# Weight rebuild through the idle accumulator bank, scaled v of the first batch on ScalarE, key low parts on VectorE

## The chip, the cores and the metric

The kernel runs on one core of a Trainium2 chip. The metric is the device time of one execution in microseconds (us); the kernel before takes 1162.75 us, the median of 3 runs (1162.2 to 1163.17). The engines are called PE (matmul), DVE (VectorE), ACT (ScalarE), POOL (GpSimd) and SP, whose queue here issues every DMA.

## The reference

Two stages. The weights reach the kernel as 64-bit numbers, all else as float32; it keeps precision by splitting numbers into a high and a low 16-bit part.

```python
q_pool = q.reshape(B, H, S // 2, 2, D).mean(axis=3)          # B=8, H=8, S=1152, D=64
scores = matmul(q_pool, k.T) / sqrt(D)                        # 576 x 1152 per head
x = softmax(scores) @ v                                       # heads side by side: (8, 576, 512)
x_prev = x shifted by one row
xk = mu_k * x + (1 - mu_k) * x_prev;  xr = mu_r * x + (1 - mu_r) * x_prev
out = sigmoid(xr @ w_r) * (maximum(xk @ w_k, 0) ** 2 @ w_v)   # w_k 512 x 1024, w_v 1024 x 512, w_r 512 x 512
```

## The kernel before, in words

**Attention.** There are 64 heads, eight to a batch, and six blocks of 96 pooled queries to a head: 384 blocks. Each has its scores in one of three PSUM tiles `s0` to `s2`. A block runs round a loop: nine score matmuls against the key's high and low parts (L462), the maximum over keys (DVE, L469), its transpose (PE, L472), the second maximum (DVE, L475), the shift spread by a small matmul (PE, L477), written into the query's spare row (ACT, L480), nine matmuls that add the rest and the shift (L486), and exp into `pf` (ACT, L492), which frees the PSUM tile. POOL then takes the low half of `pf` into `pl` (L494).

Five *windows* of 128 queries a head multiply `pf` and `pl` with `vt` and `vb` (L513, L515, L520) into one PSUM bank. DVE divides by the sum (L535 to L538); after an odd head PE turns both heads (L550) and ACT copies them out to `xt` (L553). The bank is `a`; with `ALT`, odd heads of the first batch use bank `f`, which is otherwise the accumulator of the feed-forward stage.

**Preparation of a head.** Keys: ACT rounds them (`kn`, L415), the rest is the low part (L418), by POOL for the first `KN_POOL` = 8 heads and by DVE for the others; a transposing DMA makes `ks1` of them. Values: ACT and DVE make `vt` (L428, L431), POOL makes the scaled copy `vb` (L434). Queries of two heads at a time: L382 to L389.

**Weights.** The three matrices arrive as 64-bit numbers in 20 pieces of 512 columns (`st`, two buffers). A piece is rebuilt to float32 and split: ACT takes the exponent and high mantissa (`ex`, L580) and the low mantissa bits (`em`, L587), DVE shifts and joins them (L590), DVE joins the sign (L598), ACT rounds (L600), POOL takes the rest (L601). All pieces are needed by the first batch's feed-forward.

**Feed-forward.** After each batch, tiles of 256 rows: mixing (L633 to L644), products of high and low parts (L665) in bank `f`, and in the last batch in all banks; activations (L692 to L720) and the output. The products of one batch fill PE while the next batch's attention runs.

**Order.** Nothing is issued as it is written. Every operation is recorded by `op` with its engine, a duration, what it reads and writes, a due time (`key`), and for DVE and POOL whether it needs the way to SBUF that both use (`port`). `Issue.run` then plays the record, with durations stretched by `LATE` and latencies by `SLACK`, and fixes one order for each engine; engines run in this order. A change of a duration, a due time or an engine thus moves instructions everywhere. Weights are recorded ahead of all blocks and windows, so whoever writes bank `f` later waits for what the weights did in it.

Of the kernel before, what the change touches and what calls it, by code (L numbers as in the profile page):

```python
# [256 lines left out]
def kernel(  # L257
# [145 lines left out]
    def prep(n, key):  # L403
# [37 lines left out]
    def block(n, j, i, t):  # L441
# [27 lines left out]
        op("DVE", 0.967, lambda: nc.vector.tensor_reduce(mxz, grid(0, NC).rearrange("p c q -> p q c"),  # L469
                                                         axis=AX.X, op=ALU.max),  # L470
           r=[("s", z)], w=[("mx", z)], key=t)
        op("PE", 0.057, lambda: nc.tensor.matmul(s[0:QN, 0:P], mxz, identb, start=False, stop=False,  # L472
                                                 skip_group_check=True),
# [5 lines left out]
           r=[("mb", z)], w=[("s", z)], key=t + O_MAX)  # L479
        op("ACT", 0.133, lambda: nc.scalar.activation(qlo[QN:QN + 1], s[QN:QN + 1, 0:QN], AF.Prelu,  # L480
                                                      scale=1.0 - EPS, alpha=(1.0 + EPS) / (1.0 - EPS)),
# [10 lines left out]
        op("ACT", NC * QN / 1200 + 0.051, lambda: nc.scalar.activation(  # L492
            pf[:, :, rows], grid(0, NC), AF.Exp, bias=SHIFT, scale=0.125 / (2.0 * SQ)), r=[("s", z)], w=[("pf", j)], key=t + O_EXP)
        op("POOL", NC * QN / 1000 + 0.12, lambda: nc.gpsimd.tensor_scalar(  # L494
            pl[:, :, rows], half(pf, U16, 0)[:, :, rows], LO, 1.0, op0=ALU.mult, op1=ALU.mult),
           r=[("pf", j)], w=[("pl", j)], key=t + O_REST)

    def window(n, w, t):
# [57 lines left out]


    def weights(n, w, kc, key, step):
        cols = w.shape[1]
        wv = w.bitcast(I32).rearrange("(c p) (f t) -> c p f t", p=P, t=2)  # L560
        for c in range(kc):
            for f in range(0, cols, 512):
# [17 lines left out]
                op("ACT", 0.48, lambda e=e, wh=wh: nc.scalar.activation(e, wh.bitcast(F32), AF.Abs, scale=2.0 ** -111),  # L580
                   r=[ks], w=[ke], key=key)
# [227 lines left out]
```

## Time and profile before

| what | value |
|---|---|
| runs | 1162.2, 1162.75, 1163.17 us |
| profiled execution: time, span | 1164.27 us, 1162.5 us |
| granted PE clock, mean | 0.997 |
| PE, DVE, ACT, POOL busy, share of span | 96%, 78%, 76%, 47% |
| PE's tenths in the first six of 40 slices (29 us each) | 4, 8, 8, 7, 7, 9, and 9 from there to the last but one |

Each row of a group names line, engine, operation, output and inputs by the program's names, count, busy time in us and mean in ns, then the idle time of the engine just ahead of these instructions and what ended it. A row of a stretch gives busy time and, in brackets, the number of instructions of each engine. Rows of consecutive instructions can overlap a little, and a busy PE isn't PE at its peak, since matmuls are pipelined.

### The profile page before, as it was taken

The page shows a single profiled execution, that of the slowest core. Times are in us where ns is not written, and L with a number is a line of the kernel's source. Part 1 is how long each engine was busy: PE and PEld are TensorE (multiplying, and loading weights), DVE is VectorE, ACT ScalarE, POOL GpSimd, SP SyncE. Part 2 cuts the span into 40 slices and gives each one's busy share as a digit, 9 for nine tenths or more (in the row PEclk, how much of TensorE's full clock was granted, in tenths as well). Part 3 has the DMA queues.
Part 4 walks back from the last instruction along what each step waited for, and adds up shares of the span by engine and source line. Part 5 has one row for each costly group of instructions (what it writes and reads, how often), then busy time and mean ns, then how long its engine had stood idle before and what let it go on. Part 6 is the DMA issues. An engine that isn't in the chain of part 4 may idle for free.

```text
span 1162.5 us, 45688 instructions
## 1 busy us (share of the span) xinstructions
PE 1111.6 (96%) x19504; PEld 926.0 (80%) x19504; DVE 908.2 (78%) x1791; ACT 888.7 (76%) x1838; POOL 550.0 (47%) x565
## 2 busy tenths in 40 slices
PE   4887799999999999999999999999999999999998
PEld 3776687978788887988788888979797978888565
DVE  6898878888888878888888878787888788774530
ACT  4988797887878788778877787878778778765743
POOL 4787554544445453544444453535354545443111
PEclk9999999999999999999999999999999999999999
DMA  9956663565545363564355536455554445310000
GB/s 233 219 143 175 155 135 78 134 130 126 129 99 114 94 143 98 134 123 106 90 109 120 132 81 145 85 117 115 113 123 86 95 112 93 70 30 10 20 19 28
DMA packets 222380, 126.69 MB, mean 109 GB/s; under 512 B 157664, under 2 KB 194528, under 8 KB 222176
## 3 DMA queue, kind: packets, MB, share of 16 engines
q1 hardware_dynamic: 222176, 123.77, 47.1%
q8 instruction: 152, 2.49, 0.9%
q14 instruction: 52, 0.43, 0.1%
HBM read 67.11 MB, written 9.44 MB: 66 GB/s over the span
## 4 chain that ended last, share of the span: by engine, by line
PE 85%; ACT 6%; DVE 3%; DMA 2%; issue 2%; POOL 1%; SPq 0%; DVEq 0%; ACTq 0%
PE f L665 33%; PE s L462 11%; PE s L486 11%; PE a L520 6%; PE a L515 6%; PE a L513 6%; PE s L665 4%; ACT pf L492 2%; PE s L472 2%; PE a L665 2%; DVE mx L469 1%; PE s L477 1%; PE a L550 1%; DMA st<-in_moe_w_k_dram 1%; ACT qT L480 1%
## 5 line engine op out<-in xcount | busy, mean ns | idle before, releaser
L494 POOL TENSOR_SCALAR pl<-pf 128x864 f16<-128x864 uint16 x384 | 385.0, 1003 | 405.4 <-ACT pf L492 378.3
L469 DVE TENSOR_REDUCE mx<-s 128x96 f16<-128x864 f32 x384 | 401.5, 1054 | 102.7 <-PE s L462 59.9
L492 ACT ACTIVATE pf<-s 128x864 int32<-128x864 f32 x384 | 337.4, 890 | 70.5 <-PE s L486 45.8
L462 PE MATMUL s<-qT,ks 128*128 128x96 f16 x3456 | 221.2, 207 | 28.6 <-DMA qT<-qn 15.1
L462 PEld LDWEIGHTS <-ks 128*128 128x128 f16 x3456 | 185.5, 99 | 54.6 <-issue 22.9
L515 PE MATMUL a<-vt,pf 128*128 128x64 f16 x2700 | 227.6, 194 | 0.0
L513 PE MATMUL a<-vt,pf 128*128 128x65 f16 x2700 | 227.2, 193 | 0.0
L486 PE MATMUL s<-qT,ks 128*128 128x96 f16 x3456 | 214.5, 207 | 7.2 <-ACT qT L480 6.7
L513 PEld LDWEIGHTS <-pf 128*128 128x128 f16 x2880 | 204.1, 99 | 6.0 <-ACT pf L492 0.4
L486 PEld LDWEIGHTS <-ks 128*128 128x128 f16 x3456 | 180.9, 98 | 28.5 <-issue 7.7
L515 PEld LDWEIGHTS <-pf 128*128 128x128 f16 x2880 | 194.8, 98 | 7.8 <-issue 0.3
L480 ACT ACTIVATE qT<-s 1x96 f16<-1x96 f32 x384 | 91.9, 243 | 99.8 <-PE s L477 87.6
L475 DVE TENSOR_REDUCE mb<-s 96x1 f16<-96x128 f32 x384 | 108.6, 285 | 57.9 <-PE s L472 53.3
L520 PE MATMUL a<-vb,pl 128*128 128x65 f16 x2700 | 143.4, 193 | 0.5 <-POOL pl L494 0.5
L665 PE MATMUL f<-xhk,wk_hi 128*128 128x256 f16 x496 | 135.1, 272 | 1.3 <-ACT xt L553 0.8
L665 PE MATMUL f<-xhk,wk_lo 128*128 128x256 f16 x496 | 135.1, 272 | 0.0
L665 PE MATMUL f<-xlk,wk_hi 128*128 128x256 f16 x496 | 135.1, 272 | 0.0
L520 PEld LDWEIGHTS <-pl 128*128 128x128 f16 x2880 | 121.8, 98 | 7.9 <-POOL pl L494 1.2
L696 POOL TENSOR_TENSOR gl<-g 128x512 f16<-128x512 f32 x72 | 78.5, 1090 | 100.7 <-ACT g L694 98.3
L665 PEld LDWEIGHTS <-wk_hi 128*128 128x128 f16 x1152 | 106.2, 98 | 11.6 <-issue 1.5
L472 PE MATMUL s<-identb,mx 128*96 128x128 f16 x384 | 87.1, 227 | 4.9 <-DVE mx L469 4.5
L665 PE MATMUL f<-wv_hi,g 128*128 128x512 f16 x240 | 90.9, 379 | 0.3 <-ACT ex L713 0.2
(101 smaller groups left out, 1990.2 us busy)
## 6 DMA issues: line engine op xcount, KB each, us to landing
kr<-in_k_dram SPq DMA_DIRECT2D x64, 288.0 KB, 3.3
vr<-in_v_dram SPq DMA_DIRECT2D x64, 288.0 KB, 3.1
qr<-in_q_dram SPq DMA_DIRECT2D x32, 320.0 KB, 3.7
ks<-ks SPq DMA_DIRECT2D x64, 144.0 KB, 2.8
out_dram<-em SPq DMA_DIRECT2D x36, 256.0 KB, 2.4
qr<-in_q_dram SPq DMA_DIRECT2D x32, 256.0 KB, 3.4
st<-in_moe_w_k_dram SPq DMA_DIRECT2D x8, 512.0 KB, 4.9
st<-in_moe_w_v_dram SPq DMA_DIRECT2D x8, 512.0 KB, 4.1
```

Source lines behind the costliest of these rows:

```text
L462: nc.tensor.matmul(cols(c, c + 1), ks1[hp][:, c, :], qhi, start=(c == c0), stop=False, skip_group_check=True)
L469: op("DVE", 0.967, lambda: nc.vector.tensor_reduce(mxz, grid(0, NC).rearrange("p c q -> p q c"), axis=AX.X, op=ALU.max), r=[("s", z)], w=[ ...
L472: op("PE", 0.057, lambda: nc.tensor.matmul(s[0:QN, 0:P], mxz, identb, start=False, stop=False, skip_group_check=True), r=[("mx", z)], w=[( ...
L475: op("DVE", 0.199, lambda: nc.vector.tensor_reduce(mbz[0:QN], s[0:QN, 0:P], axis=AX.X, op=ALU.max), r=[("s", z)], w=[("mb", z)], key=t + O ...
L480: op("ACT", 0.133, lambda: nc.scalar.activation(qlo[QN:QN + 1], s[QN:QN + 1, 0:QN], AF.Prelu, scale=1.0 - EPS, alpha=(1.0 + EPS) / (1.0 - ...
L486: nc.tensor.matmul(cols(c, c + 1), ks2[hp][:, c, :], qlo, start=False, stop=True, skip_group_check=True)
L492: op("ACT", NC * QN / 1200 + 0.051, lambda: nc.scalar.activation(pf[:, :, rows], grid(0, NC), AF.Exp, bias=SHIFT, scale=0.125 / (2.0 * SQ) ...
L494: op("POOL", NC * QN / 1000 + 0.12, lambda: nc.gpsimd.tensor_scalar(pl[:, :, rows], half(pf, U16, 0)[:, :, rows], LO, 1.0, op0=ALU.mult, o ...
L513: nc.tensor.matmul(bank[:, a0:a0 + VN], half(pf, F16, 1)[:, c, rows], vt[jv][:, c, D:D + VN], start=(w == 0 and c == 0), stop=False, skip_ ...
L515: nc.tensor.matmul(bank[:, a0:a0 + D], half(pf, F16, 1)[:, c, rows], vt[jv][:, c, 0:D], start=False, stop=False, skip_group_check=True)
L520: nc.tensor.matmul(bank[:, a0:a0 + VN], pl[:, c, rows], vb[jv][:, c, 0:VN], start=False, stop=(c == NC - 1), skip_group_check=True)
L665: nc.tensor.matmul(ps, terms[i][0], terms[i][1], start=(first and i == 0), stop=(i == last), skip_group_check=True)
```

## The change

It is one edit of the numbers and engines that the order is made from.

- *Rebuild* (`DEC_K`, `DEC_RV` from "D" to "S"): ACT writes the first part into bank `f` (`f_b`) instead of `ex`; DVE shifts and joins in place there (L607 in the new numbering), and joins the sign from `st` and `f` into `ex` (L610). Each of the two DVE instructions so has one operand in PSUM and one in SBUF, and both are recorded as not needing the common way. There were two `ex` buffers; there is one bank `f`.
- *Window sums* (`ALT` from 1 to 0): all heads use bank `a`.
- *Key low parts* (`KN_POOL` from 8 to 0): by DVE for all heads.
- *Scaled v* (`VB_ACT` = 8): by ACT for the first eight heads.
- *Order*: `LATE` 0.08 to 0.04, `SLACK` 0.1 to 0.05, and most of the recorded durations a little longer. All engines' orders come out anew; the instructions on PE are the same in number and kind.

```diff
--- before.py
+++ after.py
@@ -46,10 +46,12 @@
-LATE, SLACK = 0.08, 0.1
-KN_POOL, VT_POOL, XL_POOL = 8, 0, 0
-DEC_K, DEC_RV = "D", "D"
-ALT = 1
+LATE, SLACK = 0.04, 0.05
+KN_POOL, VT_POOL, XL_POOL = 0, 0, 0
+DEC_K, DEC_RV = 'S', 'S'
+ALT = 0
+PL_ENG, PL_N = (), 0
+VB_ACT = 8
 QSPLIT = 1
@@ -431,9 +433,13 @@
-        op("POOL", 0.75, lambda: nc.gpsimd.tensor_scalar(
-            vb[j][:, :, 0:D], vr[i], SV, VLO, op0=ALU.mult, op1=ALU.mult),
-           r=[("vr", i)], w=[("vb", j)], key=key + 4)
+        if n < VB_ACT:
+            op("ACT", NC * D / 1200 + 0.093, lambda: nc.scalar.activation(
+                vb[j][:, :, 0:D], vr[i], AF.Copy, scale=SV * VLO), r=[("vr", i)], w=[("vb", j)], key=key + 4)
+        else:
+            op("POOL", 0.75, lambda: nc.gpsimd.tensor_scalar(
+                vb[j][:, :, 0:D], vr[i], SV, VLO, op0=ALU.mult, op1=ALU.mult),
+               r=[("vr", i)], w=[("vb", j)], key=key + 4)
@@ -463,13 +469,13 @@
-            op("PE", (c1 - c0) * 0.0424, lambda c0=c0, c1=c1: scores(c0, c1),
+            op("PE", (c1 - c0) * 0.0430, lambda c0=c0, c1=c1: scores(c0, c1),
...
-        op("ACT", 0.133, lambda: nc.scalar.activation(qlo[QN:QN + 1], s[QN:QN + 1, 0:QN], AF.Prelu,
+        op("ACT", 0.153, lambda: nc.scalar.activation(qlo[QN:QN + 1], s[QN:QN + 1, 0:QN], AF.Prelu,
@@ -577,20 +589,49 @@
                 dec = DEC_K if n == "k" else DEC_RV
+                if dec in "STU":
+                    ep, kf = f_b.bitcast(I32), ("f",)
+                    pt = dec == "U"
+                    op("ACT", 0.52, lambda wh=wh: nc.scalar.activation(f_b, wh.bitcast(F32), AF.Abs, scale=2.0 ** -111),
+                       r=[ks], w=[kf], key=key)
+                    op("ACT", 0.565, lambda mi=mi, wl=wl: nc.scalar.activation(
+                        mi, wl.bitcast(U32), AF.Copy, scale=2.0 ** -29 * (1.0 - 2.0 ** -18), bias=-0.5 + 7.5 * 2.0 ** -18),
+                       r=[ks], w=[km], key=key)
...
+                    else:
+                        v_(0.6, lambda mi=mi, ep=ep: nc.vector.scalar_tensor_tensor(
+                            ep, ep, 3, mi, op0=ALU.logical_shift_left, op1=ALU.bitwise_or), [kf, km], [kf], False)
+                        kd, ed = (ke, e) if dec == "S" else (kf, f_b)
+                        v_(0.6, lambda ep=ep, wh=wh, ed=ed: nc.vector.scalar_tensor_tensor(
+                            ed.bitcast(I32), wh, -0x80000000, ep, op0=ALU.bitwise_and, op1=ALU.bitwise_or), [ks, kf], [kd], False)
+                    op("ACT", 0.52, lambda hi=hi, ed=ed: nc.scalar.copy(hi, ed), r=[kd], w=[("w", n, c, f)], key=key)
...
+                    else:
+                        op("POOL", 1.24, lambda lo=lo, ed=ed, hi=hi: nc.gpsimd.tensor_tensor(lo, ed, hi, op=ALU.subtract),
+                           r=[kd, ("w", n, c, f)], w=[("wl", n, c, f)], key=key)
+                    key += step
+                    continue
-                op("ACT", 0.48, lambda e=e, wh=wh: nc.scalar.activation(e, wh.bitcast(F32), AF.Abs, scale=2.0 ** -111),
+                op("ACT", 0.565, lambda e=e, wh=wh: nc.scalar.activation(e, wh.bitcast(F32), AF.Abs, scale=2.0 ** -111),
                    r=[ks], w=[ke], key=key)
```

Three places of the order, buffer numbers behind the names. First, DVE between the 39th and the 40th reduction (`mx`) of the kernel before, eleven pieces and the 40th; L590 and L598 are the rebuild, L431 `vt`, L636 and L644 the mixing:

```order
L431 SCALAR_TENSOR_TENSOR vt_85<-vr_72,vt_85 128x5x64
L590 SCALAR_TENSOR_TENSOR ex_121<-ex_121,em_123 128x512
L431 SCALAR_TENSOR_TENSOR vt_85<-vr_72,vt_85 128x4x64
L598 SCALAR_TENSOR_TENSOR ex_121<-st_125,ex_121 128x512
L636 SCALAR_TENSOR_TENSOR xm_106<-xt_102,mu_k,tmp_119 128x256
L590 SCALAR_TENSOR_TENSOR ex_120<-ex_120,em_122 128x512
L431 SCALAR_TENSOR_TENSOR vt_86<-vr_73,vt_86 128x5x64
L598 SCALAR_TENSOR_TENSOR ex_120<-st_124,ex_120 128x512
L636 SCALAR_TENSOR_TENSOR xm_105<-xt_102,mu_k,tmp_119 128x256
L644 TENSOR_TENSOR xlk_108<-xm_106,xhk_110 128x256
L431 SCALAR_TENSOR_TENSOR vt_86<-vr_73,vt_86 128x4x64
L469 TENSOR_REDUCE mx_93<-s_132 128x96
```

and the same place, from just ahead of the 39th reduction to the 40th, after the change (L475 and L481 are the two maxima, L607 and L610 the rebuild, L420 the key low part, L677 the mixing):

```order
L420 TENSOR_TENSOR kn_77<-kr_71,kn_77 128x4x64
L610 SCALAR_TENSOR_TENSOR ex_120<-st_124,f 128x512
L475 TENSOR_REDUCE mx_95<-s_134 128x96
L677 SCALAR_TENSOR_TENSOR xm_106<-xt_102,mu_k,tmp_119 128x256
L481 TENSOR_REDUCE mb_97<-s_133 96x1
L420 TENSOR_TENSOR kn_77<-kr_71,kn_77 128x5x64
L607 SCALAR_TENSOR_TENSOR f<-f,em_123 128x512
L481 TENSOR_REDUCE mb_98<-s_134 96x1
L547 TENSOR_SCALAR den_100<-a 128x5
L610 SCALAR_TENSOR_TENSOR ex_121<-st_125,f 128x512
L475 TENSOR_REDUCE mx_93<-s_132 128x96
```

What stood in a row is spread between the maxima of three blocks; the key low parts have come in.

Second, POOL at its first pieces, before and after (L494 and L506 are `pl`, L418 the key low part, L434 `vb`, L601 and L617 the rebuild's rest):

```order
L434 TENSOR_SCALAR vb_90<-vr_72 128x9x64
L494 TENSOR_SCALAR pl<-pf 128x9x96 x3
L418 TENSOR_TENSOR kn_77<-kr_71,kn_77 128x4x64
L418 TENSOR_TENSOR kn_77<-kr_71,kn_77 128x5x64
L494 TENSOR_SCALAR pl<-pf 128x9x96 x3
L601 TENSOR_TENSOR wk_lo<-ex_121,wk_hi 128x512
L494 TENSOR_SCALAR pl<-pf 128x9x96 x2
L601 TENSOR_TENSOR wk_lo<-ex_120,wk_hi 128x512
```

```order
L506 TENSOR_SCALAR pl<-pf 128x9x96 x9
L617 TENSOR_TENSOR wk_lo<-ex_121,wk_hi 128x512
L506 TENSOR_SCALAR pl<-pf 128x9x96
L617 TENSOR_TENSOR wk_lo<-ex_120,wk_hi 128x512
L506 TENSOR_SCALAR pl<-pf 128x9x96 x3
L617 TENSOR_TENSOR wk_lo<-ex_121,wk_hi 128x512
```

Only `pl` and the rebuild's rest are left there.

Third, DVE after the change where the last two pieces of the rebuild stand, at the 55th to 57th reduction:

```order
L475 TENSOR_REDUCE mx_93<-s_132 128x96
L607 SCALAR_TENSOR_TENSOR f<-f,em_123 128x512
L685 TENSOR_TENSOR xlk_108<-xm_106,xhk_110 128x256
L610 SCALAR_TENSOR_TENSOR ex_121<-st_125,f 128x512
L481 TENSOR_REDUCE mb_96<-s_132 96x1
L475 TENSOR_REDUCE mx_94<-s_133 128x96
L607 SCALAR_TENSOR_TENSOR f<-f,em_122 128x512
L475 TENSOR_REDUCE mx_95<-s_134 128x96
L610 SCALAR_TENSOR_TENSOR ex_120<-st_124,f 128x512
L481 TENSOR_REDUCE mb_97<-s_133 96x1
```

On PE the first feed-forward matmul (L706) stands behind the 55th block's second scores. In the kernel before it stood behind the 50th's, eight of them by the 51st, and four of the 20 pieces of the rebuild came behind DVE's 54th reduction.

More of the change, by code (lines that the diff above doesn't have):

```diff
@@ L465, in block @@
         for c0, c1 in BK:
-            op("PE", (c1 - c0) * 0.0424, lambda c0=c0, c1=c1: scores(c0, c1),
+            op("PE", (c1 - c0) * 0.0430, lambda c0=c0, c1=c1: scores(c0, c1),
                r=[("ks1", hp)] + kh, w=[("s", z)], key=t)
-        op("DVE", 0.967, lambda: nc.vector.tensor_reduce(mxz, grid(0, NC).rearrange("p c q -> p q c"),
+        op("DVE", 0.975, lambda: nc.vector.tensor_reduce(mxz, grid(0, NC).rearrange("p c q -> p q c"),
                                                          axis=AX.X, op=ALU.max),
            r=[("s", z)], w=[("mx", z)], key=t)
-        op("PE", 0.057, lambda: nc.tensor.matmul(s[0:QN, 0:P], mxz, identb, start=False, stop=False,
+        op("PE", 0.059, lambda: nc.tensor.matmul(s[0:QN, 0:P], mxz, identb, start=False, stop=False,
                                                  skip_group_check=True),
@@ L489, in block @@
         for c0, c1 in BK:
-            op("PE", (c1 - c0) * 0.0424, lambda c0=c0, c1=c1: scores2(c0, c1),
+            op("PE", (c1 - c0) * 0.0430, lambda c0=c0, c1=c1: scores2(c0, c1),
                r=[("ks2", hp)] + kl, w=[("s", z)], key=t + O_EXP)
-        op("ACT", NC * QN / 1200 + 0.051, lambda: nc.scalar.activation(
+        op("ACT", NC * QN / 1200 + 0.06, lambda: nc.scalar.activation(
             pf[:, :, rows], grid(0, NC), AF.Exp, bias=SHIFT, scale=0.125 / (2.0 * SQ)), r=[("s", z)], w=[("pf", j)], key=t + O_EXP)
-        op("POOL", NC * QN / 1000 + 0.12, lambda: nc.gpsimd.tensor_scalar(
-            pl[:, :, rows], half(pf, U16, 0)[:, :, rows], LO, 1.0, op0=ALU.mult, op1=ALU.mult),
-           r=[("pf", j)], w=[("pl", j)], key=t + O_REST)
+        pe = PL_ENG[i % len(PL_ENG)] if i < PL_N else "POOL"
+        if pe == "ACT":
+            op(pe, NC * QN / 1200 + 0.09, lambda: nc.scalar.activation(
+                pl[:, :, rows], half(pf, U16, 0)[:, :, rows], AF.Copy, scale=LO), r=[("pf", j)], w=[("pl", j)], key=t + O_REST)
+        else:
+            en, d = (nc.gpsimd, NC * QN / 1000 + 0.12) if pe == "POOL" else (nc.vector, NC * QN / 1920 + 0.07)
+            op(pe, d, lambda: en.tensor_scalar(
+                pl[:, :, rows], half(pf, U16, 0)[:, :, rows], LO, 1.0, op0=ALU.mult, op1=ALU.mult),
+               r=[("pf", j)], w=[("pl", j)], key=t + O_REST, port=True)
     def window(n, w, t):
@@ L550, in turned @@
                     nc.tensor.transpose(bank[:, r_:r_ + P], xz[:, k_].rearrange("p h d -> p (h d)"), ident)
-            op("PE", 0.11 * (k1 - k0), turned, r=[("xb", 0), ("xb", 1)], w=[ka], key=t + O_TURN)
+            op("PE", 0.113 * (k1 - k0), turned, r=[("xb", 0), ("xb", 1)], w=[ka], key=t + O_TURN)
             op("ACT", 0.051 + (qe - q0) / 1200, lambda q0=q0, qe=qe, base=base: nc.scalar.copy(
@@ L586, in weights @@
                 else:
-                    op("ACT", 0.48, lambda mi=mi, wl=wl: nc.scalar.activation(
+                    op("ACT", 0.565, lambda mi=mi, wl=wl: nc.scalar.activation(
                         mi, wl.bitcast(U32), AF.Copy, scale=2.0 ** -29 * (1.0 - 2.0 ** -18), bias=-0.5 + 7.5 * 2.0 ** -18),
@@ L592, in weights @@
                 if dec == "P":
-                    op("ACT", 0.48, lambda sz=sz, wh=wh: nc.scalar.activation(sz, wh.bitcast(F32), AF.Sign),
+                    op("ACT", 0.565, lambda sz=sz, wh=wh: nc.scalar.activation(sz, wh.bitcast(F32), AF.Sign),
                        r=[ks], w=[kz], key=key)
@@ L688, in ff @@
                               (wlo["k"][:, c, fs], hk[:, c, 0:n], r)]
-                products(pv[:, f - f0], pk, terms, n / 2400.0 + 0.0019, first=(f == f0))
+                products(pv[:, f - f0], pk, terms, n / 2400.0 + 0.0025, first=(f == f0))
             z = turn("r32")
```

14 lines of the change are left out of this document (12 added, 2 removed).

## The prediction

> **What bounds the kernel now.** I read three views in turn: the busy times by stretch, PE's waits, and PE's timeline where the waits stop. Cut at 149.7 us, the stretches are:
>
> ```profile
> core 0: us, PE busy (x) PEld busy (x) DVE busy (x) ACT busy (x) POOL busy (x), PEclk, DMA share, GB/s
> 16.10:149.70 133.60, 105.83 (x2228) 95.39 (x2227) 115.59 (x207) 110.94 (x218) 89.69 (x87) 0.97 0.74 179
> 300.00:1060.00 760.00, 758.28 (x13869) 642.14 (x13868) 623.02 (x1239) 597.13 (x1244) 361.45 (x370) 1.00 0.47 104
> ```
>
> From 300 us on PE is busy 99.8% of the time; nothing another engine does there can show. Before 149.7 us PE idles, and the busiest are DVE (115.6 of 133.6, 87%) and ACT (83%). PE's two largest waits of the whole run, and then the largest of 150 to 1070 us:
>
> ```profile
> PE s L462 <- DMA qT<-qn: 15.1, 1, 15.1
> PE s L462 <- ACT pf L492: 13.0, 28, 1.4
> ...
> PE s L462 <- ACT pf L492: 0.9, 4, 0.3
> ```
>
> The loop is scores, maximum (DVE), its transpose, second maximum (DVE), shift (ACT), second scores, exp (ACT), over three score banks; PE waits until ACT has emptied a bank. The change of regime in PE's timeline, and two prices for PE's pieces:
>
> ```profile
> 149.72 0.27 PE L665 MATMUL f<-xhk,wk_lo 128*128 128x256 f16 x1
> 149.83 0.27 PE L665 MATMUL f<-xhk,wk_hi 128*128 128x256 f16 x1
> ...
> 155.85 0.55 PE L486 MATMUL s<-qT,ks 128*128 128x96 f16 x9
> 156.23 0.55 PE L462 MATMUL s<-qT,ks 128*128 128x96 f16 x9
> 156.66 0.19 PE L513 MATMUL a<-vt,pf 128*128 128x65 f16 x1
> 156.69 0.19 PE L515 MATMUL a<-vt,pf 128*128 128x64 f16 x1
> ```
>
> From 149.72 feed-forward matmuls (L665) fill every hole. PE's work is the same before and after the change, so **the time moves by what PE idles before that point**, and nothing else that I see.
>
> **A third resource: DVE against POOL.** Groups of this stretch, DVE and POOL, and then the shortest, median and longest of three of them up to 160 us:
>
> ```profile
> L590 DVE SCALAR_TENSOR_TENSOR ex<-ex,em 128x512 int32<-128x512 int32 x16 | 12.3, 770 | 0.4 <-ACT ex L580 0.4
> L598 DVE SCALAR_TENSOR_TENSOR ex<-st,ex 128x512 int32<-128x512 int32 x16 | 11.2, 697 | 0.0
> L431 DVE SCALAR_TENSOR_TENSOR vt<-vr,vt 128x256 f16<-128x256 f32 (+1 forms) x15 | 9.6, 646 | 0.0
> L636 DVE SCALAR_TENSOR_TENSOR xm<-xt,mu_k,tmp 128x256 f32<-128x256 f32 x4 | 3.0, 738 | 0.0
> ...
> L494 POOL TENSOR_SCALAR pl<-pf 128x864 f16<-128x864 uint16 x52 | 53.4, 1027 | 26.2 <-ACT pf L492 22.9 <-POOL wk_lo L601 0.5
> L418 POOL TENSOR_TENSOR kn<-kr,kn 128x256 f16<-128x256 f32 (+1 forms) x10 | 9.1, 927 | 0.5
> L601 POOL TENSOR_TENSOR wr_lo<-ex,wr_hi 128x512 f16<-128x512 f32 x4 | 6.7, 1668 | 4.9 <-ACT wr_hi L600 4.8
> ```
>
> ```profile
> L590 DVE SCALAR_TENSOR_TENSOR ex<-ex,em x18: 674/682/1639, 30.4 to 155.3; 128x512 int32<-128x512 int32 x18
> L431 DVE SCALAR_TENSOR_TENSOR vt<-vr,vt x16: 410/484/1179, 22.8 to 151.6; 128x320 f16<-128x320 f32 x8, 128x256 f16<-128x256 f32 x8
> L494 POOL TENSOR_SCALAR pl<-pf x53: 912/913/1986, 22.1 to 156.0; 128x864 f16<-128x864 uint16 x53
> ```
>
> Medians are steady, but single ones take about 1 us more, the length of one POOL piece. The timelines, POOL's rows first, show why: a POOL piece of 1.16 us takes 2.29 while DVE's pieces pass, and the DVE piece after them takes 1.38 where it has 0.47 elsewhere.
>
> ```profile
> 102.13 1.16 POOL L601 TENSOR_TENSOR wr_lo<-ex,wr_hi 128x512 f16<-128x512 f32 x1
> 106.57 2.29 POOL L601 TENSOR_TENSOR wr_lo<-ex,wr_hi 128x512 f16<-128x512 f32 x1 [3.29 <-ACT wr_hi L600]
> ...
> 106.16 0.69 DVE L590 SCALAR_TENSOR_TENSOR ex<-ex,em 128x512 int32<-128x512 int32 x1
> 107.16 0.68 DVE L598 SCALAR_TENSOR_TENSOR ex<-st,ex 128x512 int32<-128x512 int32 x1
> 107.76 1.38 DVE L636 SCALAR_TENSOR_TENSOR xm<-xt,mu_k,tmp 128x256 f32<-128x256 f32 x1
> ...
> 114.20 0.47 DVE L636 SCALAR_TENSOR_TENSOR xm<-xt,mu_k,tmp 128x256 f32<-128x256 f32 x1
> ```
>
> A DVE piece with two SBUF inputs and a POOL piece exclude each other. Mean less median, times count, gives DVE's waits: L590 16 x 0.09 = 1.4, L598 (by L590's median) 0.3, L431 15 x 0.16 = 2.4, and L636 4 x 0.27 = 1.1 against its 0.47: **5.2 us**. POOL's come to 52 x 0.114 = 5.9 in L494, 4 x 0.51 = 2.0 in L601 and some 2 in L418. Without waits POOL (89.7 busy) holds the way for 80 us and DVE's two-input pieces for 35 (32 of the rebuild at 0.60, 43 small ones at about 0.37): 115 of 133.6 us, **86%**.
>
> **The change, part by part, up to PE's filling point.** In the new order feed-forward starts later in the program: the rebuild works in the bank that it accumulates in, so all twenty pieces must be through DVE first.
>
> *DVE.* Two reductions in a row cost 0.97 each:
>
> ```profile
> 16.11 2.02 DVE L469 TENSOR_REDUCE mx<-s 128x96 f16<-128x864 f32 x2 [1.40 <-PE s L462]
> ```
>
> so a row overlaps its successor by 0.08, and a rebuild instruction takes 0.682 - 0.08 = 0.60. Counting DVE's order from its first reduction to the 54th (before) and to the last rebuild instruction (after): three reductions of each kind more, 2.9 + 0.6; eight rebuild instructions more (40 against 32), 4.8; ten key low parts more, 3.65; three `vt` fewer, since they moved into the start, -1.05. Sum **+10.9 us**. Of the 5.2 us of waits the rebuild's 1.7 go if an operand outside SBUF frees it from POOL; the way's use then falls to 55 `pl` x 0.913 + 20 x 1.16 + 2 `vb` on POOL and 49 small DVE pieces, some 93 us, 69%. I let 1.5 of 5.2 stay (bounds 0 and 5.2). DVE then needs 115.6 + 10.9 - 3.7 = 122.8 us.
>
> *The PSUM operand.* Nearest rows, an all-SBUF instruction and one that reads PSUM, later in the run:
>
> ```profile
> L720 DVE SCALAR_TENSOR_TENSOR ex<-ex,em x22: 648/679/694, 307.3 to 962.0; 128x512 f32<-128x512 f32 x22
> L729 DVE SCALAR_TENSOR_TENSOR em<-f,ex x22: 680/692/693, 314.6 to 971.1; 128x512 f32<-128x512 f32 x22
> ```
>
> 13 ns by 40 is 0.5 us. No row writes PSUM from DVE, so the upper bound is that a piece stays as dear as L590's mean, 0.77: 40 x 0.09 = 3.5 us. I take 0, since the median of the PSUM row is the nearest.
>
> [...]
>
> *ACT.* Three exps (1.67 for two in a row, so 0.78 each), six rebuild activations, three casts, and five of the eight `vb` in this stretch (three lie before it): 2.4 + 6 x 0.60 + 3 x 0.52 + 5 x 0.57. The rows, from the timeline, from durations up to 160 us and from the groups:
>
> ```profile
> 22.55 1.67 ACT L492 ACTIVATE pf<-s 128x864 int32<-128x864 f32 x2
> ...
> L580 ACT ACTIVATE ex<-st x18: 653/684/697, 29.7 to 153.9; 128x512 f32<-128x512 f32 x18
> L385 ACT ACTIVATE qn<-qs x9: 613/631/739, 15.8 to 159.6; 128x512 f16<-128x512 f32 x5, 128x640 f16<-128x640 f32 x4
> ...
> L600 ACT CAST wk_hi<-ex 128x512 f16<-128x512 f32 x8 | 4.9, 616 | 0.7 <-DVE ex L598 0.6
> ```
>
> Each is taken less an overlap of 0.08 to 0.1, and `vb`, with 576 columns, between the 512 and 640 of L385. That is **+10.5**, to 121.4. An Abs that writes PSUM is priced as one that writes SBUF; its bounds, a tenth of a microsecond either way by the spread of these rows, make 2 us in all.
>
> *PE.* It has done more when feed-forward starts: six runs of nine scores at 0.385, 48 + 27 window matmuls at 0.03, five small ones, less eight L665 at 0.11: 2.3 + 2.3 + 0.3 - 0.9 = **4.0 us**, which come off. So with the start unchanged the stretch may last 137.6 us for no change.
>
> *Start.* POOL's key low parts, on DVE now, release the first transpose sooner, at most 0.9 us by POOL's rows; but the chain there runs through a transfer, its row second. I take 0.4 (bounds 0 and 0.9).
>
> ```profile
> 5.93 0.71 POOL L418 TENSOR_TENSOR kn<-kr,kn 128x256 f16<-128x256 f32 x1
> ...
> 8.44 3.27 DMA kr<-in_k_dram
> ```
>
> *One window bank instead of two.* The window sums of the next head now wait until the pair before is divided, turned and copied out. Now a turn costs PE, behind the third pair (shifts stand behind the copies on ACT),
>
> ```profile
> 107.74 2.02 PE L486 MATMUL s<-qT,ks 128*128 128x96 f16 x27 [2.56 <-ACT qT L480]
> ```
>
> 2.56 us; four such would be 10, none is the other bound. I take no change, since every head from the ninth on already has one bank and PE is full there.
>
> **What share can DVE hold?** It holds 87% now; its fuller slices:
>
> ```profile
> 60.00:70.00 10.00, 8.64 (x209) 7.79 (x207) 9.13 (x16) 9.74 (x19) 7.38 (x9) 1.00 0.40 104
> 100.00:110.00 10.00, 6.18 (x116) 5.47 (x114) 9.51 (x20) 7.46 (x18) 6.31 (x7) 0.91 0.74 193
> ```
>
> The way's use falls by 17 points, and the new order spreads the DVE pieces that the old one bunches where POOL idles. Bounds 87% and 93%; I take 91%, as in the first slice. 122.8 / 0.91 = 134.9, or +1.3; less 4.0 and 0.4 gives **-3.1 us**. The profiled execution took 1164.27, so 1161.2 by it; it lies 1.5 above the median of the runs, 1162.75, hence **1159.7**.
>
> [...]
>
> **Rivals.** (1) *ACT becomes the pace*, slower. Place: exp and shift queue behind the five `vb` and the three further rebuild pieces ahead of feed-forward. For: 83% now, and 121.4 us in 134.9 would be 90%, a share it reaches only in slices. Against: the slice at 60 us has 9.74. At 85.5% the stretch lasts 142 us: +8.4 - 4.4 = +4.0, 1166.8. It decides once ACT can't hold 121.4 / 138 = 88%. If neither DVE's share nor its waits improve either, (115.6 + 10.9) / 0.87 = 145.4 gives +7.4, 1170.2. (2) *The way isn't freed*, no measurable change: the rebuild still excludes POOL, or its pieces stay as dear as now, and the waits stay. For: no row shows DVE working in place in PSUM. Against: the longest L729 is 693 ns, though so is L720's, with two SBUF inputs. 126.5 / 0.91 = 139.0, +5.4 - 4.4 = +1.0, 1163.8.
>
> **How the numbers follow.** Forecast 43%, rival 1 33%, rival 2 24% (within 0.2%, 2.3 us, about what a measurement of this kernel tells from no change). So faster 0.43, same 0.24, slower 0.33; the likeliest case's own range is 1154 to 1160.4. Low end: all waits gone, 93% and the whole start, 121.3 / 0.93 = 130.4, -3.2 - 4.9 = -8.1, 1154.6, rounded to 1154 for ACT's bound. High end: between rival 1 and its worst, 1168.
>
> **What would show it.** Right: L607 and L610 with longest near median; POOL's `pl` mean near 0.95; DVE's share from its first reduction to the first L706 above 90%, that stretch under 137 us; PE full behind it. Wrong: ACT below 88% there with DVE's idle time ending on ACT; rows of L607 above 0.75; or PE idle after that point, which I hold at nothing.

## The result, and the profile after

| kernel | median of runs, us | lowest to highest | profiled execution: time, span |
|---|---|---|---|
| before | 1162.47 | 1162.0 to 1163.17 | 1164.27, 1162.5 |
| changed | 1168.67 | 1166.98 to 1170.64 | 1168.09, 1165.9 |

The change is slower by half a per cent: ratio 1.0052, 95% interval 1.004 to 1.0065. The two profiled executions are 3.4 us of span apart, the medians 6.2, since the one of before lay above its median and the one of the change a little below. The traces are compared with each other, so 3.4 us is what they have to account for; the other 2.8 us of the medians are not in them.

Ahead of PE's filling point the change did what it says. Durations from the trace of the changed kernel up to 160 us (shortest, median, longest, in ns), and then the groups of 16 to 152.5 us:

```profile
L607 DVE SCALAR_TENSOR_TENSOR f<-f,em x20: 677/688/700, 33.2 to 150.2; 128x512 int32<-128x512 int32 x20
L610 DVE SCALAR_TENSOR_TENSOR ex<-st,f x20: 642/675/689, 33.9 to 151.8; 128x512 int32<-128x512 int32 x20
L595 ACT ACTIVATE f<-st x20: 605/634/672, 30.8 to 149.5; 128x512 f32<-128x512 f32 x20
```

```profile
L506 POOL TENSOR_SCALAR pl<-pf 128x864 f16<-128x864 uint16 x55 | 53.0, 964 | 61.1 <-ACT pf L498 55.4 <-DVE mb L481 2.0 <-DVE kn L420 1.6
...
L595 ACT ACTIVATE f<-st 128x512 f32<-128x512 f32 x20 | 12.7, 636 | 0.0
...
L617 POOL TENSOR_TENSOR wr_lo<-ex,wr_hi 128x512 f16<-128x512 f32 x4 | 4.9, 1228 | 4.7 <-ACT wr_hi L612 4.6
```

No rebuild piece waits for POOL any more (the longest is 0.70 us, where L590 had 1.64), `pl` fell from 1027 to 964 ns and the rebuild's rest `wr_lo` from 1668 to 1228 ns. The first feed-forward matmul comes at 152.5 us, and PE has done more in the first 200 us. Busy times by stretch, of before and then of the change:

```profile
0.00:200.00 200.00, 155.69 (x3013) 135.64 (x3014) 165.67 (x310) 160.85 (x319) 124.44 (x129) 0.98 0.69 165
200.00:1060.00 860.00, 857.33 (x15769) 729.24 (x15768) 708.34 (x1415) 676.79 (x1412) 409.32 (x421) 1.00 0.48 106
600.00:1060.00 460.00, 459.24 (x8412) 390.95 (x8410) 371.05 (x735) 358.51 (x743) 220.43 (x225) 1.00 0.45 98
```

```profile
0.00:200.00 200.00, 160.18 (x3080) 140.37 (x3081) 167.75 (x338) 168.47 (x334) 101.86 (x107) 0.96 0.73 173
200.00:1060.00 860.00, 855.76 (x15642) 725.01 (x15639) 711.46 (x1396) 673.01 (x1398) 402.15 (x418) 1.00 0.48 104
600.00:1060.00 460.00, 458.56 (x8346) 388.38 (x8344) 371.56 (x720) 354.68 (x732) 210.03 (x223) 1.00 0.45 96
15.90:152.50 136.60, 112.16 (x2356) 102.01 (x2354) 118.99 (x226) 120.99 (x233) 77.04 (x77) 0.94 0.76 184
```

Up to 200 us PE got through 67 matmuls more; from 200 to 1060 us it got through 127 fewer, though it reads 99.5% busy, and of 19504 it has some 60 more left at 1060 than the kernel before. So the loss lies where the prediction held PE to be full. The granted clock there is 1.00 in both, so a slower clock is not the reason.

**A finer measure.** The busy time of PE rounds such holes away, because the ends of matmuls are modelled. Their starts are not. So the distance from the start of each row of PE's timeline to the start of the next is taken, less the row's count times the usual distance of its kind (medians: scores 0.0428, window sums 0.030, feed-forward 0.109 and 0.216, turn 0.11, maximum's transpose 0.058, shift 0.047 us). What is left are *gaps*. With PE's start they give the span in every profile below: span less (start plus all gaps) is 1086.1 to 1086.8 us in all 18 kernels. That is PE's work, which is the same in all, and the short end behind it. Distances between starts add up to the span by construction; what the small spread shows is that the usual distances hold in every kernel, so that what differs between kernels is the start and the gaps.

| us | before | changed |
|---|---|---|
| PE's start | 15.1 | 15.05 |
| gaps up to 200 us | 53.0 | 50.0 |
| gaps from 200 to 1060 us (number over 0.1 us) | 8.0 (27) | 14.6 (49) |
| gaps behind | 0.1 | 0.1 |
| sum | 76.3 | 79.7 |

3.1 us were won before 200 us, and 6.5 lost behind. One of the larger gaps in the changed kernel, PE's rows and then ACT's:

```profile
536.30 0.38 PE L492 MATMUL s<-qT,ks 128*128 128x96 f16 x5
...
537.32 0.38 PE L706 MATMUL f<-wv_hi,gl 128*128 128x512 f16 x1
537.54 0.49 PE L562 MATMUL a<-ident,xb 128*128 128x128 f32 x3
538.58 0.54 PE L468 MATMUL s<-qT,ks 128*128 128x96 f16 x9 [0.55 <-ACT pf L498]
...
536.88 0.74 ACT L387 ACTIVATE qn<-qs 128x640 f16<-128x640 f32 x1
537.64 1.67 ACT L498 ACTIVATE pf<-s 128x864 int32<-128x864 f32 x2
```

The second scores of a block are done at 536.68, but its exp, the first of the two in the last row, stands behind a rounding of queries in ACT's order and starts at 537.64. PE's order holds one feed-forward matmul and three transposes ahead of the scores that need the bank; then it stands for 0.55 us, since the order is fixed. Most gaps are 0.1 to 0.4 us, and the view of waits, of PE from 200 to 1060 us, has 14 entries where the gaps over 0.1 us are 49. Its largest three give 1.9 us for the exp, against 0.9 in the kernel before:

```profile
PE s L468 <- ACT pf L498: 1.9, 8, 0.6
PE s L492 <- ACT qT L486: 0.6, 3, 0.2
PE s L483 <- DVE mb L481: 0.2, 1, 0.2
```

### The profile page after: what moved, and what is told of

Its sections match the earlier page's. It is cut to its first block, busy times and chain, and to the rows that moved or that the text cites. A ratio compares the mean times of both kernels' runs of the same rounds, so it can differ in the third digit from the quotient of the medians.

```text
span 1165.9 us, 45668 instructions
## 1 busy us (share of the span) xinstructions
PE 1118.0 (96%) x19504; PEld 929.8 (80%) x19504; DVE 915.3 (79%) x1807; ACT 895.6 (77%) x1846; POOL 521.4 (45%) x541
## 4 chain that ended last, share of the span: by engine, by line
PE 66%; ACT 3%; DVE 1%; issue 1%; ACTq 0%; DVEq 0%
PE f L706 26%; PE s L492 8%; PE s L468 8%; PE a L532 5%; PE a L527 5%; PE a L525 5%; PE s L706 4%; PE a L706 2%; PE s L478 1%; ACT pf L498 1%; PE s L483 1%; PE a L562 1%; DVE mx L475 0%; ACT qT L486 0%; ACT r L733 0%
## 5 line engine op out<-in xcount | busy, mean ns | idle before, releaser
L506 POOL TENSOR_SCALAR pl<-pf 128x864 f16<-128x864 uint16 x384 | 374.9, 976 | 456.0 <-ACT pf L498 429.6
L475 DVE TENSOR_REDUCE mx<-s 128x96 f16<-128x864 f32 x384 | 400.2, 1053 | 109.6 <-PE s L468 70.5
L468 PE MATMUL s<-qT,ks 128*128 128x96 f16 x3456 | 225.9, 208 | 31.0 <-ACT pf L498 15.2
L525 PE MATMUL a<-vt,pf 128*128 128x65 f16 x2880 | 243.9, 193 | 1.1 <-ACT xt L565 0.6
L527 PE MATMUL a<-vt,pf 128*128 128x64 f16 x2880 | 244.4, 194 | 0.0
L468 PEld LDWEIGHTS <-ks 128*128 128x128 f16 x3456 | 187.6, 99 | 54.7 <-issue 26.2
L492 PE MATMUL s<-qT,ks 128*128 128x96 f16 x3456 | 218.2, 208 | 3.7 <-ACT qT L486 3.4
L492 PEld LDWEIGHTS <-ks 128*128 128x128 f16 x3456 | 184.4, 99 | 28.6 <-issue 7.6
L532 PE MATMUL a<-vb,pl 128*128 128x65 f16 x2880 | 153.5, 193 | 0.0
L481 DVE TENSOR_REDUCE mb<-s 96x1 f16<-96x128 f32 x384 | 108.3, 284 | 42.4 <-PE s L478 36.0
L706 PE MATMUL f<-xhk,wk_hi 128*128 128x256 f16 x496 | 135.1, 272 | 0.3 <-ACT r L733 0.2
L706 PE MATMUL f<-xhk,wk_lo 128*128 128x256 f16 x496 | 135.1, 272 | 0.0
L706 PE MATMUL f<-xlk,wk_hi 128*128 128x256 f16 x496 | 135.1, 272 | 0.0
L737 POOL TENSOR_TENSOR gl<-g 128x512 f16<-128x512 f32 x72 | 81.8, 1137 | 104.5 <-ACT g L735 102.1
L532 PEld LDWEIGHTS <-pl 128*128 128x128 f16 x2880 | 121.4, 98 | 5.3 <-POOL pl L506 0.2
L706 PEld LDWEIGHTS <-wk_hi 128*128 128x128 f16 x1152 | 106.2, 98 | 10.6 <-issue 0.6
L706 PE MATMUL f<-wv_hi,g 128*128 128x512 f16 x240 | 90.9, 379 | 0.8 <-ACT ex L754 0.3
```

The source lines that it names most:

```text
L468: nc.tensor.matmul(cols(c, c + 1), ks1[hp][:, c, :], qhi, start=(c == c0), stop=False, skip_group_check=True)
L475: op("DVE", 0.975, lambda: nc.vector.tensor_reduce(mxz, grid(0, NC).rearrange("p c q -> p q c"), axis=AX.X, op=ALU.max), r=[("s", z)], w=[ ...
L481: op("DVE", 0.199, lambda: nc.vector.tensor_reduce(mbz[0:QN], s[0:QN, 0:P], axis=AX.X, op=ALU.max), r=[("s", z)], w=[("mb", z)], key=t + O ...
L492: nc.tensor.matmul(cols(c, c + 1), ks2[hp][:, c, :], qlo, start=False, stop=True, skip_group_check=True)
L506: op(pe, d, lambda: en.tensor_scalar(pl[:, :, rows], half(pf, U16, 0)[:, :, rows], LO, 1.0, op0=ALU.mult, op1=ALU.mult), r=[("pf", j)], w= ...
L525: nc.tensor.matmul(bank[:, a0:a0 + VN], half(pf, F16, 1)[:, c, rows], vt[jv][:, c, D:D + VN], start=(w == 0 and c == 0), stop=False, skip_ ...
```

## The experiments

All times are medians beside runs of the kernel before on the same chip, with the ratio to it.

### Which part of the change makes the gaps

> The changed kernel with LATE and SLACK at 0.08 and 0.1 again, as before the change; all else as changed. Margins (the narrower margin lets PE meet its semaphores a little late in the part that is full of work, 6.6 us between 200 and 1060 us): those holes go back to about the 8 us of the kernel before, and the gain of about 2.6 us ahead of 200 us stays, so 1160 to 1163 us. Durations (the longer recorded durations are to blame) and edits (the moved pieces are): no change, 1167 to 1170. Draw (every new order falls differently by some microseconds): anything from 1160 to 1170.

```diff
-LATE, SLACK = 0.04, 0.05
+LATE, SLACK = 0.08, 0.1
```

1163.34 us, ratio 1.0009 (0.9998 to 1.002). Gaps behind 200 us: 9.7 us, 26 over 0.1. The front kept its gain (14.7 + 50.7 = 65.4 us). The time is what margins expected to within 0.4 us, the gaps are 1.7 us more than the 8 that it named.

> The kernel before with LATE and SLACK at 0.04 and 0.05 and nothing else changed. Margins: the holes behind 200 us grow from 8 to 14 us, and the time to 1167 to 1170. Durations and edits: no change, 1162 to 1163. Draw: anything from 1160 to 1170.

```diff
-LATE, SLACK = 0.08, 0.1
+LATE, SLACK = 0.04, 0.05
```

1175.74 us, ratio 1.011 (1.0097 to 1.0123). Gaps behind 200 us: 16.6 us, 52 over 0.1, where 14 were expected. The time went beyond every range that was named: gaps were 2.6 us more than expected, and PE's start moved too, from 15.1 to 16.75 us.

> The changed kernel, margins 0.04 and 0.05, with the recorded durations of all operations that both kernels have as they were before the change. Durations: back to 1160 to 1163. Margins: no better, 1167 to 1171, since recorded durations that are too short narrow the margin further. Edits: 1167 to 1170. Draw: anything from 1160 to 1170.

```diff
-            op("PE", (c1 - c0) * 0.0430, lambda c0=c0, c1=c1: scores(c0, c1),
+            op("PE", (c1 - c0) * 0.0424, lambda c0=c0, c1=c1: scores(c0, c1),
...
-        op("DVE", 0.975, lambda: nc.vector.tensor_reduce(mxz, grid(0, NC).rearrange("p c q -> p q c"),
+        op("DVE", 0.967, lambda: nc.vector.tensor_reduce(mxz, grid(0, NC).rearrange("p c q -> p q c"),
```

The other recorded durations go back likewise. 1171.05 us, ratio 1.0071 (1.0059 to 1.0083); 15.1 us of gaps, 41 over 0.1. The longer recorded durations are not the cause.

> The rebuild through the idle bank, one window bank, key low parts on VectorE and scaled v on ScalarE alone; margins and recorded durations as before the change. Margins and durations: 1158 to 1162, the gain ahead of 200 us without the holes behind it, or part of it. Edits: 1167 to 1170. Draw: anything from 1160 to 1170.

To the durations of the third experiment comes

```diff
-LATE, SLACK = 0.04, 0.05
+LATE, SLACK = 0.08, 0.1
```

1161.99 us, ratio 0.9989 (0.998 to 0.9997): a small gain. The front is the best so far, 11.9 + 50.4 = 62.3 us against 68.1 before, but the back has 11.2 us of gaps, 32 over 0.1. So the edits themselves don't make the time longer.

### Margins, or the luck of an order

The order starts from due times with a random part, so each edit could simply draw another order. Wider margins and another seed were to show how far orders spread.

> The changed kernel with LATE and SLACK at 0.12 and 0.15, all else as changed. Margins: PE's gaps between 200 and 1060 us, 14.6 us at 0.04 and 9.7 at 0.08, fall a little further, to 6 to 9; 1159 to 1163 us as long as the wider margin costs nothing ahead of the filling point. Draw (the three pairs of margins so far fell by chance): 1160 to 1172, gaps anywhere from 8 to 17 us.

> The kernel before with LATE and SLACK at 0.12 and 0.15 and nothing else. Margins: gaps between 200 and 1060 us of 8 us or less (8.0 at 0.08, 16.6 at 0.04); 1160 to 1164 us. Draw: 1160 to 1172, gaps anywhere from 8 to 17 us.

In place of 0.04 and 0.05 in the changed kernel, and of 0.08 and 0.1 in the one before:

```diff
+LATE, SLACK = 0.12, 0.15
```

1172.34 us for the changed kernel, ratio 1.008 (1.0067 to 1.0094), and 1179.85 for the one before, 1.0144 (1.013 to 1.0158). Gaps behind 200 us: 12.8 (37) and 12.0 (36). Wider isn't better, against what margins expected. Both times lie above the range of draw too, since the kernel before lost 12 us in the front and the changed one 5.

> The kernel before with the seed of its order's random start at 1 instead of 2; margins, durations and work the same. Margins: within 2 us of 1162.5, gaps between 200 and 1060 us of 7 to 11. Draw: off by 4 us or more, gaps that differ from 8.0 as much as they did between the margins (4 to 9 us).

> The changed kernel with the seed at 1 instead of 2, margins 0.04 and 0.05 as changed. Margins: 1167 to 1172, gaps between 200 and 1060 us of 13 to 17. Draw: off by 4 us or more from 1168.7, gaps down to 8.

```diff
-SEED, SPREAD = 2, 1.0
+SEED, SPREAD = 1, 1.0
```

Before: 1179.86 us, ratio 1.0148 (1.0134 to 1.0162); the changed kernel: 1173.59, 1.0087 (1.0071 to 1.0102). Another seed alone, with the same work, engines and margins, costs the kernel before 17 us: 9.9 in the front (13.1 + 64.9 = 78.0 against 68.1) and 5.2 in the back (13.2, 32 over 0.1). That is what draw expected. The kernel before is a good draw among those tried. The changed kernel has 14.5 us in the back, 54 over 0.1: the gaps are where margins expected them, the time, 4.9 us further, is where draw did.

Four kernels with the narrow margin now had 41 to 54 gaps, five with the middle one (one of them below, the rebuild alone) 26 to 34. So the same two kernels were run with the seed held and only the margin changed.

> The changed kernel with seed 1 and margins 0.08 and 0.1; its pair with 0.04 and 0.05 and the same seed had 54 gaps over 0.1 us between 200 and 1060 us, 14.5 us in all. Margins: 26 to 36 gaps, 8 to 13 us. Draw: the number falls anywhere, 26 to 54, 8 to 17 us. The time depends on the front as well and says less.

> The kernel before with seed 1 and margins 0.04 and 0.05; its pair with 0.08 and 0.1 and the same seed had 32 gaps over 0.1 us between 200 and 1060 us, 13.2 us in all. Margins: 40 gaps or more, 14 to 17 us. Draw: anywhere from 26 to 54, 8 to 17 us.

The changed kernel, seed 1, margins 0.08 and 0.1: 1164.77 us, ratio 1.0012 (1.0003 to 1.0021), with 23 gaps and 8.4 us in the back, from 54 and 14.5. The kernel before, seed 1, margins 0.04 and 0.05: 1179.69, ratio 1.0139 (1.0126 to 1.0153), with 46 gaps and 14.9 us, from 32 and 13.2. The first has fewer gaps even than margins expected (26 to 36), the second is as expected but moves only a little. By their microseconds both also lie within the wide range of draw. What speaks against draw is that all five pairs that differ in the margin alone go the same way: 8.0 us of gaps with the middle margin and 16.6 with the narrow one, 9.7 and 14.6, 11.2 and 15.1, 8.4 and 14.5, 13.2 and 14.9. All kernels planned as a whole, by margin:

| margin | gaps from 200 to 1060 us | number over 0.1 us |
|---|---|---|
| 0.04, 0.05 (5 kernels) | 14.5 to 16.6, mean 15.1 | 41 to 54 |
| 0.08, 0.1 (7 kernels) | 8.0 to 13.2, mean 10.6 | 23 to 38 |
| 0.12, 0.15 (2 kernels) | 12.0, 12.8 | 36, 37 |

The narrow and the middle one don't overlap. How the margin gets into the order can be counted from PE's row of matmuls with the distances above: between a block's shift and its second scores (time for ACT's piece between them) the tightest twentieth of blocks 68 to 371 has less than 0.81 or 0.82 us of other PE work in the seven kernels with 0.08, less than 0.71 to 0.75 in the five with 0.04, and less than 0.86 in the two with 0.12. So the margin sets how much work PE has at hand at this place while the block goes round. The gaps just ahead of second scores go with it: between 200 and 1060 us they make 2.4 to 4.6 us in the five kernels with the narrow margin, 0.7 to 2.0 in the seven with the middle one, 1.3 and 1.1 with the widest. They are the smaller part. The other gaps, many of them ahead of a block's first scores, make 10.6 to 12.1, 6.1 to 11.3, and 11.2 and 10.3 us: on the whole fewer with the middle margin, but the groups overlap, and the widest margin doesn't lower them. What makes these was not followed up, so why the widest margin isn't better stays open.

### The order alone

Both kernels record equally many operations in the same sequence, so the order of one can be continued by the order of the other: what isn't issued yet at the cut follows in the other's order.

```diff
-        for n in best[1]:
+        done = set(best[1][:CUT])
+        for n in best[1][:CUT] + [n for n in BACK if n not in done]:
```

`CUT` is the number of operations taken from the kernel's own order, and `BACK` the other order, a long list of numbers that is left out here.

> The changed kernel up to about 200 us (its own first 1636 operations, some 68 blocks), and from there all operations in the order that the kernel before issues them. Back order (the loss lies in the order behind the filling point, whatever made it): gaps between 200 and 1060 us fall from 14.6 to 8 or 9, time from 1168.7 to 1161 to 1164. State (what the edits leave behind, for example fuller buffers or a slower clock, makes the same back slower): gaps stay at 12 to 15, 1166 to 1169.

1161.83 us, ratio 0.9984 (0.9976 to 0.9993). Gaps behind 200 us: 7.9 us, 26 over 0.1.

> The four edits with margins and recorded durations as before the change (1162.0 us) for the first 1636 operations, and behind them the order of the kernel before. Back order: gaps between 200 and 1060 us fall from 11.2 to 8 or 9, time 1157.5 to 1160.5, faster than both kernels. State: 1161 to 1163.

1157.68 us, ratio 0.9952 (0.994 to 0.9965): faster than both kernels. Gaps 8.5 us, 26 over 0.1; front 11.6 + 49.6 = 61.2 us.

> The kernel before for its first 1636 operations, without any of the four edits, and behind them the order that the changed kernel has. Back order: gaps between 200 and 1060 us grow from 8.0 to 13 to 15, time from 1162.5 to 1167 to 1170. State: no change, 1162 to 1164.

1173.43 us, ratio 1.0083 (1.007 to 1.0097), some 3 us beyond the expected range. Gaps 16.5 us, 52 over 0.1. From 600 us on they are those of the changed kernel, 6.6 us; from 200 to 600 us, where the seam is, they are 9.9 against its 8.0.

The stretches from 600 us on show it without any working out. They were given above for the kernel before (459.24) and for the change (458.56). With the back of before behind the changed front, and then the back of the change behind the front of before:

```profile
600.00:1060.00 460.00, 459.48 (x8389) 390.37 (x8387) 371.43 (x735) 357.60 (x743) 221.02 (x226) 1.00 0.45 97
```

```profile
600.00:1060.00 460.00, 458.57 (x8336) 388.28 (x8333) 372.58 (x725) 355.05 (x734) 209.63 (x223) 1.00 0.45 98
```

And one stretch of 100 us of each, in the sequence before, changed, changed front with the back of before, front of before with the changed back:

```profile
700.00:800.00 100.00, 100.00 (x1852) 85.69 (x1850) 81.91 (x162) 78.72 (x164) 47.52 (x49) 1.00 0.53 115
```

```profile
700.00:800.00 100.00, 99.59 (x1817) 84.36 (x1814) 82.83 (x162) 78.50 (x162) 45.25 (x49) 1.00 0.51 115
```

```profile
700.00:800.00 100.00, 100.00 (x1846) 85.77 (x1843) 81.46 (x159) 78.20 (x163) 47.74 (x50) 1.00 0.55 114
```

```profile
700.00:800.00 100.00, 99.58 (x1812) 83.56 (x1809) 84.43 (x162) 76.54 (x158) 43.77 (x48) 1.00 0.49 113
```

PE's busy time goes with the order of the back, not with the kernel ahead of it: 100.00 for the one, 99.6 for the other. The theory called state, that the edits leave something behind which slows the rest, falls.

> Three pieces of order: the edits with margins and durations as before the change for the first 1688 operations (some 72 blocks), the order of the changed kernel with margins 0.08 and 0.1 up to the 2696th (about 300 us, where it had 0.6 us of gaps between 200 and 300 us against 2.0 to 2.9), and the order of the kernel before behind it (5.9 us of gaps from 300 us on). If gaps belong to the piece of order: start and gaps of 62.3 + 0.6 + 5.9 + 0.1 = 69 us or a little less, against 69.7 in the kernel of two pieces that took 1157.7: 1156 to 1157.5 us. If pieces disturb each other: 1158 to 1161.

1156.9 us, ratio 0.995 (0.9936 to 0.9964). Start and gaps 68.9 us, 69 expected; the back has 7.5 us, 24 over 0.1. It is the fastest kernel of this study, though by the intervals not to be told from the one of two pieces that took 1157.68 us.

### What pays in the front

> The rebuild through the idle bank and one window bank alone; key low parts stay on POOL and scaled v on POOL for the first eight heads, margins and recorded durations as before the change. Its order comes out anew, so the time can fall by several us either way; what counts is PE's start and gaps up to 200 us, 68.1 us in the kernel before and 62.3 with all four edits. If the rebuild is what pays: 62 to 65. If the moved pieces pay: 67 or more. In either case the rebuild's instructions on DVE stay near 0.68 us at the longest.

Against the kernel with the four edits alone:

```diff
-KN_POOL, VT_POOL, XL_POOL = 0, 0, 0
+KN_POOL, VT_POOL, XL_POOL = 8, 0, 0
...
-VB_ACT = 8
+VB_ACT = 0
```

1160.58 us, ratio 0.9972 (0.9961 to 0.9982). Start and gaps up to 200 us: 12.15 + 50.4 = 62.6 us.

> The key low parts on VectorE and the scaled v of the first eight heads on ScalarE alone; rebuild and window banks, margins and recorded durations as before the change. If the rebuild is what pays in the front: PE's start and gaps up to 200 us stay at 67 us or more (68.1 before, 62.6 with the rebuild alone, 62.3 with all four edits). If the moves pay too: 65 or less.

Against the same kernel:

```diff
-DEC_K, DEC_RV = 'S', 'S'
-ALT = 0
+DEC_K, DEC_RV = 'D', 'D'
+ALT = 1
```

1171.93 us, ratio 1.0073 (1.006 to 1.0085). Start and gaps up to 200 us: 15.8 + 55.4 = 71.2 us. The groups up to 160 us, first with the rebuild alone, then with the moves alone:

```profile
L607 DVE SCALAR_TENSOR_TENSOR f<-f,em 128x512 int32<-128x512 int32 x20 | 13.8, 689 | 0.4 <-ACT f L595 0.2
L610 DVE SCALAR_TENSOR_TENSOR ex<-st,f 128x512 int32<-128x512 int32 x20 | 13.5, 673 | 0.0
```

```profile
L639 DVE SCALAR_TENSOR_TENSOR ex<-st,ex 128x512 int32<-128x512 int32 x18 | 12.9, 719 | 0.0
L631 DVE SCALAR_TENSOR_TENSOR ex<-ex,em 128x512 int32<-128x512 int32 x18 | 12.7, 708 | 0.2 <-ACT em L628 0.2
```

Shortest, median and longest of these, in the same sequence:

```profile
L607 DVE SCALAR_TENSOR_TENSOR f<-f,em x20: 681/686/700, 33.1 to 148.9; 128x512 int32<-128x512 int32 x20
L610 DVE SCALAR_TENSOR_TENSOR ex<-st,f x20: 644/674/687, 33.9 to 149.7; 128x512 int32<-128x512 int32 x20
```

```profile
L631 DVE SCALAR_TENSOR_TENSOR ex<-ex,em x18: 650/682/1184, 30.5 to 156.7; 128x512 int32<-128x512 int32 x18
L639 DVE SCALAR_TENSOR_TENSOR ex<-st,ex x18: 675/681/1378, 31.3 to 157.5; 128x512 int32<-128x512 int32 x18
```

With the rebuild in the bank no piece is long, though POOL kept all of its work; with POOL's work moved off and the rebuild in SBUF long ones remain. The same holds in all 18 profiles: the longest of the 40 pieces takes 0.70 us in each of the eleven kernels with the rebuild in the bank, and 1.07 to 1.65 us in the seven without. So it is the place of the operand, and not the other moves, that frees these pieces from POOL.

With margins, durations and seed the same, the front is 68.1 us without any edit, 62.6 with the rebuild alone, 71.2 with the moves alone and 62.3 with both. One order each settles little where a seed moves the front by 9.9 us, but six pairs of one margin and one seed point the same way: with the rebuild the front is shorter by 3.3 us (margin alone on the kernel before, against the changed kernel with the old durations), 5.5 (before, against the rebuild alone), 6.9 and 9.9 (seed 1, narrow and middle margin), 8.9 (moves alone, against all four edits) and 10.2 (widest margin). Only in the pairs of 5.5 and 8.9 is the rebuild, with the one window bank that goes with it, all that differs; the others have the moves in them too. For the moves no gain is seen, beside the rebuild (62.3 against 62.6) or alone. Of the 5.5 us, 3.0 are an earlier start of PE; starts fell anywhere between 11.5 and 16.9 us in these orders, with and without the rebuild, and what sets them was not followed up.

## Why the prediction was wrong

It forecast 1159.7 us; the change takes 1168.67, outside its range.

**The step that failed** is the sentence on which the sum rests, that the time moves by what PE idles before the filling point, "and nothing else that I see". PE's idle time behind it was held at nothing and grew by 6.5 us, the last of the signs that the prediction named for being wrong. The quoted stretch of before had PE at 758.28 of 760 us, and I took that as full. It wasn't: the start-to-start distances give that kernel 8.0 us of gaps from 200 to 1060 us, and other orders of the same work up to 16.6. The edit that did it, `LATE` and `SLACK`, stands in the diff, and the prediction has no term for it. Put back alone, it takes the gaps from 14.6 to 9.7 us and the median from 1168.67 to 1163.34; the remaining 1.7 us are no more than orders with one margin differ by (8.0 to 13.2), and the kernel before has the fewest gaps of its seven. That the order is what counts, and nothing else that the edits leave behind, is shown by the exchanged backs: 7.9 us with the back of before behind the changed front, 16.5 the other way round.

The busy time of the weight loads (PEld) showed more of the loss than PE's: from 200 to 1060 us it moved from 729.24 to 725.01 us, where PE's moved from 857.33 to 855.76.

**The terms before the filling point** came out as follows.

- *The rebuild's instructions*: priced at the median of before, nothing dearer for PSUM. Measured 688 and 675 ns by the median, against 682: right, and so is the freeing from POOL (longest 700 and 689 ns, against 1639).
- *DVE's need*, 122.8 us, and *its share*, 91%. Measured 118.99 in 136.6 us, so 87%, as in the kernel before. Both terms were too high; their quotient, a stretch of 134.9, came out only 1.7 us short.
- *ACT*, 121.4 us: measured 120.99, in 136.6 us 88.6%. Its terms add up to 10.4, not 10.5. It held the 88% at which rival 1 was to take over, and no more. The stretch grew by 3.0 us, where 1.3 was forecast. ACT was as near to being the bound as DVE.
- *PE's work by then*, 4.0 us more: 3.9 by the counted rows (84.3 us at 149.7, 88.2 at 152.5).
- *Start*, 0.4 us: 0.07, within its bounds.
- Not in the sum: from its filling point to 200 us the kernel before still had 2.7 us of gaps, the changed one 0.8 from 152.5 us on.

So at the filling point 1.1 us were won (3.9 of work, less 2.8 by which that point came later) instead of 3.1, and at 200 us 3.1. That the latter is the number forecast is luck: the stretch grew more than twice as much as forecast, and gaps behind the filling point, which the sum didn't have, made up for it.

**The rivals.** ACT as the pace would have shown as a longer front, and the way that isn't freed as long rebuild pieces; neither came. The time lies near rival 1's worst case, 1170.2, but for a reason that isn't among the rivals: the front came out shorter, not longer. The missing rival was a new order of the part where PE is full, priced from the slack in that part. That it was possible could be seen from the change itself: it gives every engine a new order for 860 us in which nothing else is changed, with less margin.

**What stays open**: why margins of 0.12 and 0.15 don't lower the gaps further, what makes the gaps ahead of first scores, what sets PE's start, and how much of the front's differences between orders (62 to 80 us) has a cause that could be read ahead of time. The margin's effect in the back is shown in five pairs, in one of them of 1.7 us only (seed 1 of the kernel before).

## What to carry to other kernels

Where an edit goes through a planner, compare orders before edits: run the unchanged kernel with another seed, and hold the order of the untouched part fixed (here by continuing one order with the other) when judging an edit. A full engine with a fixed order still loses time in holes too short for the busy view (14.6 us here, where PE read 99.5% busy), and how much work the order leaves at hand between a request and its answer is one thing that sets them. An edit that gains 3 us in one stage can be worth nothing when the order of the other stages isn't kept.

## What the runs showed of the hardware

- Gaps repeat. The same piece of order had the same gaps behind different fronts: from 800 to 900 us 1.07, 1.17 and 1.07 us with the order of before, 1.63 and 1.61 with the changed one; from 1000 to 1060 us 0.00 to 0.04 and 1.02 twice.
- The DVE instruction that reads and writes the same PSUM tile in place (L607) takes by the median what L590 took in SBUF (688 against 682 ns), without the waits for POOL: the longest took 0.70 us against 1.64, and over all profiles 0.70 against 1.07 to 1.65.
- No delay by POOL shows in DVE's instructions with an input in PSUM, but in many with both inputs in SBUF. In the kernel before, the 64 divisions `xb` (L538), with one input in PSUM, take 476 to 493 ns and the 384 reductions `mx` (L469), from PSUM, 1040 to 1060, while the 64 `vt` of 320 columns (L431) go from 448 to 1191. Of POOL's 384 `pl` pieces (L494) the 189 that no DVE instruction with two SBUF inputs overlaps take 912 to 915 ns, and all 95 over 1 us overlap one. The traces show the delay, not what the two engines share.
- The Abs that writes PSUM (L595) takes 634 ns by the median, the one that wrote SBUF (L580) 684: 50 ns less on 512 columns.
